# Low halves of h from PSUM by VectorE, GpSimd out of the weights' split, and an earlier first unit, in an attention and two mixture-of-experts layers on one core

## The chip, the core and the metric

The kernel runs on one core of a Trainium2 chip, as one program. The time is that of one launch on the device, in microseconds (us). The core has a matmul engine (TensorE, PE in the profile; PEld is its loading of weights), VectorE (DVE), ScalarE (ACT), GpSimd (POOL) and SyncE (SP), which here only starts transfers. Each engine works through its own queue in order; semaphores tie them together. SBUF is the on-chip memory that all of them read and write, PSUM the smaller one into which matmuls write.

## The reference

Attention over chunks of 32 tokens, then two layers of experts, all in float32 from and to DRAM:

```python
x = attention(q, k, v, mem_k, mem_v)         # 4 x 8 heads x 768 tokens x 64 -> 3072 tokens x 512
# first layer: each token goes to one of 8 experts, by the largest logits first, at most 384 to each
logits = x @ w_gate
for idx in argsort(-logits.flatten()):
    tok, e = idx // 8, idx % 8
    if assigned[tok] < 0 and counts[e] < 384:
        assigned[tok] = e; counts[e] += 1
for e in range(8):
    mask = assigned == e
    out[mask] = maximum(x[mask] @ w1[e], 0) @ w2[e]      # w1[e] 512 x 1024, w2[e] 1024 x 512
# second layer: each token goes to its best two of 8 experts, by noisy logits
noisy = x @ w_gate + log1p(exp(x @ w_noise)) * noise
top2, wt = top two of noisy, softmax over the two
for e in range(8):
    out[mask] += wt * (maximum(x[mask] @ w1[e], 0) @ w2[e])
```

The two layers have weights of their own. Tokens of the first layer depend on the gates of all tokens, and the second layer's gates on the first layer's outputs.

## The kernel before

Attention takes the first 165 us or so and is not touched but for a scale. Then an order of tokens is found (`route`), and the 16 experts follow, numbered k = 0 to 15: 0 to 7 are the first layer (called experts 0 to 7 here), 8 to 15 the second, in an order that depends on their load.

**One expert.** For the first layer 384 tokens are gathered by GpSimd's indirect DMAs into `xg`, and transposed by DMA into `xT`, as two float16 parts (high and low). `mm1` (L1168) computes 8 tiles of 128 of the 1024 hidden features: each is 12 matmuls, (high, high), (high, low) and (low, high) of weights and tokens, into one of three PSUM tiles (`tile1`). For k < KF = 5, the relu `hT` stays in float32 and the second matmul is in float32 too (`mm2_f32`), from the unsplit weights. From expert 5 on `hT` is also split: ScalarE writes the relu as float32 (`ht`) and as float16 (the high part), and `halve` (L1155) subtracts the two on GpSimd, or on VectorE if GpSimd is behind. `mm2` (L1205) then has 24 matmuls for each block of 128 tokens, 512 columns wide.

**The second layer.** An expert has up to 7 blocks of 128 slots, in two units: unit u = 2e with columns 0 to 3, the last a half block (448 slots), and u = 2e + 1 with columns 4 to 6 (384 slots). `lists2` and `list2` make the list of tokens of a unit by matmuls against one-hot rows (`slps<-slr,sloh`), `gathers2` fetches them, and `sums2` gathers the rows already in the output (`pv`), adds on VectorE and scatters them back. Unit 0 is special: its tokens come only from the first EARLY = 18 blocks of 128, that is the outputs of the first six experts, so that its list (`l1`) can be made while experts 6 and 7 still run. The list of unit 1 needs the gates of all 24 blocks (`M`, `rtqpos`). `gate_math` is run for the blocks in three groups: 0 to 11, 12 to 17, 18 to 23.

**Weights.** Each of the 32 weight matrices (i = 2k + m, m = 0 for w1) comes in four `st` tiles of 128 x 1024. ScalarE squares them, one matmul with ones (`tot`) makes the norm, from it VectorE makes a power-of-two scale, and `halves` (L1104) writes the high part by ScalarE and the low part in pieces: 256 columns by VectorE, or 512 by GpSimd as a multiplication and a subtraction. w2 of experts 0 to 4 is not split. In the profile these are `w_0h`, `w_0l` to `w_3h`, `w_3l`.

**What sets the order.** Nothing is placed by hand after the attention. `Pipe` (L73) keeps a modelled clock for each engine: each instruction goes through `Eng`, which adds its modelled cost in `account` (that is why all these instructions stand as L68 in the profile). The work around the matmuls is written as generators that yield a time or a condition. Between two matmuls `tick` runs each generator that is due, in the order of the list `gens`. `fits` lets VectorE take a piece when its clock is not ahead. Where PE needs something that by the model is not there, `until` and `wait` issue dummy matmuls (`m<-ones`) into the tile that is about to be used. So a changed cost in the model moves instructions on every engine.

Of the kernel before, what the change touches and what calls it, by code (L numbers as in the profile page):

```python
# [8 lines left out]
F32 = mybir.dt.float32  # L9
F16 = mybir.dt.float16  # L10
BF16 = mybir.dt.bfloat16
I32 = mybir.dt.int32
# [24 lines left out]
EARLY = CAP // 128 * (E - 2)  # L37
# [35 lines left out]
class Pipe:  # L73
# [9 lines left out]
    def __init__(self, nc):  # L83
        self.t = {k: 0.0 for k in "pvsgyd"}
        self.ready = {}
        self.due = 0.0
        self.early = set()
# [7 lines left out]
    def account(self, e, op, args, kw):  # L95
# [29 lines left out]
        elif e == "s":  # L125
            cost = (51.0 if ps else 93.0) + 94.0 * (ptr or "accum_out" in kw) + 0.833 * n
        else:
            cost = 147.0 + 1.887 * n if op == "tensor_tensor" else (245.0 if ptr else 122.0) + 0.832 * n
        end = self.t[e] = start + cost
# [26 lines left out]
    def add(self, gen, first=False):  # L156
        self.gens.insert(0 if first else len(self.gens), [gen, self.clock, False, None])
# [38 lines left out]
def pow2_scale(V_, pool, ssq, n, tag, keep=6, out=None):  # L196
# [5 lines left out]
    V_.tensor_scalar(s, t, -1.0, float(204 << 23), op0=ALU.mult, op1=ALU.add)  # L202
    V_.tensor_scalar(i, t, 1.0, float(50 << 23), op0=ALU.mult, op1=ALU.add)
# [17 lines left out]
def attention(ctx):  # L221
# [3 lines left out]
    with (  # L225
# [110 lines left out]
        def split(i):  # L336
# [4 lines left out]
            sx, ix = pow2_scale(nc.vector, wk, ssq, 1, "x", out=ixs[:, i : i + 1])  # L341
# [208 lines left out]
def positions(ctx, m, tag, between=(lambda: None,) * 2, counts=None):  # L550
# [11 lines left out]
    yield pipe.rdy("p", exc)  # L562
# [414 lines left out]
C_H = 2.0**-15  # L977
# [67 lines left out]
def split(ctx, i, st, eager):  # L1045
# [18 lines left out]
    def norms(js):  # L1064
        n = js.stop - js.start
        yield pipe.rdy("p", sq) + 1000
# [10 lines left out]
            i2[:, js].bitcast(I32), t[:, js], float(23 << 23), float(50 << 23), op0=ALU.max, op1=ALU.add  # L1077
# [26 lines left out]
    def halves(j, s):  # L1104
# [12 lines left out]
        fits = pipe.fits(395.0)  # L1117
        idle = lambda: (k == 0 or KF <= k <= E) and pipe.t["g"] <= pipe.clock + SLACKG
        a = 0
        while a < 1024:  # L1120
            yield lambda: fits() or idle()
            b = a + 256 if fits() else min(a + 512, 1024)
            if b == a + 256:
# [21 lines left out]
    if not eager:  # L1145
        s = yield from norms(slice(0, 4))
        if k < E:
            for j in reversed(range(4)):
                pipe.add(halves(j, s), True)
# [5 lines left out]
def halve(ctx, h, t, n, hT):  # L1155
    pipe = ctx.pipe
    yield pipe.rdy("g", h)
    fits = pipe.fits(69.0 + 1.04 * n)
    yield lambda: pipe.t["g"] <= pipe.clock + SLACKH or fits()
    (pipe.G if pipe.t["g"] <= pipe.clock + SLACKH else pipe.V).tensor_tensor(h[:, 1, :n], t, h[:, 0, :n], op=ALU.subtract)  # L1160
    hT.append(h)
# [6 lines left out]
def mm1(ctx, k, xT, n, ps, last=True):  # L1168

    pipe, W, hT = ctx.pipe, ctx.W[k], []  # L1170
    for ft in range(FT):
        if ft:
            ps = tile1(ctx)
# [20 lines left out]
        else:  # L1194
            t = ctx.wk.tile([128, n], F32, tag="ht", name="ht", bufs=3)
# [789 lines left out]
```

## Time and profile before

| | us |
|---|---|
| median of 3 runs | 1122.9 |
| lowest and highest | 1116.53 and 1127.39 |
| profiled execution, its own time | 1120.83 |
| its span in the trace | 1119.0 |
| mean granted clock of TensorE | 0.946 |
| attention and order of tokens, to the first expert's first matmul | 191.57 |
| experts 0 to 4, float32 second matmul | 229.92 |
| experts 5, 6, 7 | 40.20, 35.66, 48.67 |
| units 0, 1, 2 of the second layer | 53.07, 32.86, 43.34 |
| from unit 3 to the third last | 336.15 |
| last three units | 93.20 |
| tail | 14.36 |

The stages are cut at the first matmul of each expert or unit. Durations below are of the one profiled execution. [...] An idle time in brackets stands for the engine just before the instruction, with the instruction that it waited for.

### The profile page before, as it was taken

The numbers are of one execution on the slowest core, as the hardware profiler recorded it, in microseconds if no ns is written. First come the engines' busy times: TensorE is split into PE (matmuls) and PEld (weight loads), VectorE is DVE, ScalarE is ACT, GpSimd is POOL, SyncE is SP. The second block draws the span as 40 slices with busy tenths as digits, with TensorE's granted clock in tenths as the row PEclk, the third lists the DMA queues.
The fourth block names the chain that finished last, engine by engine and source line by source line (L and its number), as shares of the span: only waits on it lengthen the run. The fifth ranks groups of instructions, "written<-read, shape, count | busy, mean of one in ns | idle before, by whom it ended". The sixth has DMA issues, their size and how long they took to land. (4 is left out here: it accounts for less than half of the span.)

```text
span 1119.0 us, 21999 instructions
## 1 busy us (share of the span) xinstructions
PE 1000.2 (89%) x8051; PEld 598.2 (53%) x8051; DVE 730.9 (65%) x2337; ACT 495.0 (44%) x878; POOL 461.3 (41%) x589
## 2 busy tenths in 40 slices
PE   7767746999999998988978989999999999999994
PEld 6655634667676674444434435555455554555552
DVE  3676877878888889889685854827558374575100
ACT  1454523433524516885616815526255361643220
POOL 5455523301101225647434444544546444454531
PEclk8898966999999999998988999999999999999997
DMA  9999715456696758774538845637658364553510
GB/s 224 225 260 264 204 69 199 146 161 195 184 219 190 207 137 228 202 220 132 110 67 243 271 118 168 185 84 215 142 167 191 108 222 112 155 121 87 132 37 28
DMA packets 162657, 185.44 MB, mean 166 GB/s; under 512 B 108224, under 2 KB 120896, under 8 KB 162546
## 3 DMA queue, kind: packets, MB, share of 16 engines
q1 hardware_dynamic: 143856, 127.96, 44.6%
q0 software_dynamic: 15232, 49.75, 14.8%
q10 hardware_dynamic: 3458, 6.30, 1.6%
q8 instruction: 64, 1.05, 0.4%
q14 instruction: 47, 0.39, 0.1%
HBM read 127.14 MB, written 32.44 MB: 143 GB/s over the span
## 5 line engine op out<-in xcount | busy, mean ns | idle before, releaser
L68 PEld LDWEIGHTS <-hT 128*128 128x128 f16 (+2 forms) x1800 | 144.6, 100 | 183.4 <-issue 22.6
L68 ACT ACTIVATE ht<-m 128x384 f32<-128x384 f32 (+2 forms) x152 | 76.3, 502 | 255.0 <-PE m L68 230.6
L68 ACT ACTIVATE junk<-st 128x1024 f16<-128x1024 f32 x108 | 114.1, 1056 | 62.2 <-DVE sloh L68 22.6
L68 POOL TENSOR_TENSOR hT<-ht,hT 128x384 f16<-128x384 f32 (+2 forms) x121 | 117.2, 980 | 55.3 <-ACT hT L68 40.1
L68 DVE SCALAR_TENSOR_TENSOR pv<-m,ys,pv 128x512 f32<-128x512 f32 (+2 forms) x47 | 33.5, 714 | 148.5 <-PE m L68 148.1
L68 PE MATMUL m2f<-st,hT 128*128 128x256 f32 x480 | 124.7, 396 | 0.0
L68 POOL DMA_INDIRECT out_dram<-pv,ts x47 | 47.4, 1009 | 176.6 <-DVE pv L68 131.4
L68 POOL DMA_INDIRECT xg<-xr,idx x24 | 24.8, 1032 | 186.7 <-issue 95.4
L68 PE MATMUL m<-xT,w_3h 128*128 128x384 f16 (+2 forms) x384 | 99.6, 338 | 0.0
L68 PE MATMUL m<-xT,w_0h 128*128 128x384 f16 (+2 forms) x384 | 98.7, 337 | 0.0
L68 PE MATMUL m<-xT,w_2h 128*128 128x384 f16 (+2 forms) x384 | 97.0, 331 | 1.7 <-ACT hT L68 1.7
L68 PE MATMUL m<-xT,w_1h 128*128 128x384 f16 (+2 forms) x384 | 97.3, 333 | 0.0
L68 PEld LDWEIGHTS m2f<-st,hT 128*128 128x128 f32 x480 | 84.4, 190 | 10.0 <-ACT hT L68 0.3
L68 PE MATMUL m<-w_3h,hT 128*128 128x512 f16 (+2 forms) x300 | 72.5, 347 | 8.4 <-POOL hT L68 8.4
L68 PE MATMUL m<-w_0h,hT 128*128 128x512 f16 (+2 forms) x300 | 73.9, 354 | 2.9 <-ACT w_0h L68 2.9
L68 ACT ACTIVATE hT<-m 128x384 f16<-128x384 f32 (+2 forms) x152 | 75.9, 500 | 0.0
L68 PE MATMUL m<-w_1h,hT 128*128 128x512 f16 (+2 forms) x300 | 73.7, 351 | 0.0
L68 PE MATMUL m<-w_2h,hT 128*128 128x512 f16 (+2 forms) x300 | 73.0, 349 | 0.0
L68 DVE SCALAR_TENSOR_TENSOR w_1l<-st,s,w_1h 128x256 f16<-128x256 f32 x92 | 63.1, 728 | 13.2 <-ACT w_1h L68 13.2
L68 PE MATMUL m<-xT,w_3l 128*128 128x384 f16 (+2 forms) x192 | 65.0, 339 | 0.0
L68 PE MATMUL m<-xT,w_0l 128*128 128x384 f16 (+2 forms) x192 | 64.5, 336 | 0.0
L68 DVE SCALAR_TENSOR_TENSOR w_2l<-st,s,w_2h 128x256 f16<-128x256 f32 x102 | 61.9, 657 | 3.5 <-ACT w_2h L68 3.5
(339 smaller groups left out, 2128.1 us busy)
## 6 DMA issues: line engine op xcount, KB each, us to landing
st<-w_dram SPq DMA_DIRECT2D x64, 512.0 KB, 5.5
st<-x_dram SPq DMA_DIRECT2D x64, 512.0 KB, 4.5
v<-vctx_dram SPq DMA_DIRECT2D x24, 520.0 KB, 14.1
k<-kT_dram SPq DMA_DIRECT2D x24, 312.0 KB, 15.7
x<-rb SPq DMA_DIRECT2D x24, 264.0 KB, 2.5
q<-qT_dram SPq DMA_DIRECT2D x12, 512.0 KB, 17.4
out_dram<-zero ACTq DMA_DIRECT2D x24, 256.0 KB, 4.4
xr<-rb POOLq DMA_DIRECT2D x17, 264.0 KB, 7.6
```

Source lines behind the costliest of these rows:

```text
L68: return f(*args, **kw)
```

## The change

1. `halve`: for k from 5 on, ScalarE writes the high part only; VectorE computes max(PSUM, 0) minus the high part straight from the matmul's PSUM tile. GpSimd does it, from a float32 copy, only in the first layer when by the model VectorE is late and GpSimd free. `mm1` has a new `until`: a tile is begun only if at most two low parts are open.
2. `halves`: GpSimd takes part for k = 0 only; VectorE's pieces have 512 columns from k = 5 on.
3. `account`: a model of VectorE and GpSimd holding each other up when both work on two tensors in SBUF (`held`).
4. EARLY is 15 blocks, the outputs of five experts; the groups of `gate_math` become 0 to 8, 9 to 14, 15 to 23.
5. Order: `add` takes a rank (0 for `halve`, 1 for `halves` and the last two experts' `gate_rows`, else 2); `norms` waits 4000 ns of the model in place of 1000 for k from 5 on; the lists' matmuls of `l1` and `rtq` and the list of unit 0 and 1 come 2000 later.
6. Scales: powers of two are moved (TOPX, C_H), with no instruction more or less.

The low parts of h are 152 in number. Of these the order has 8 on GpSimd and 144 on VectorE after the change, where the profile has 121 on GpSimd and 31 on VectorE before. VectorE's weight pieces are 66 of 256 columns and 176 of 512, where 374 of 256 were; GpSimd's pairs 7 where 29 were. The dummies `m<-ones` are 106 where 55 were: 20 of the new ones stand ahead of expert 0, 31 ahead of unit 1.

```diff
-EARLY = CAP // 128 * (E - 2)
+EARLY = CAP // 128 * (E - 3)
...
+        if op in ("tensor_tensor", "scalar_tensor_tensor") and not ps:
+            if e == "g":
+                if self.t["v"] > start:
+                    start += 200.0
+                    self.t["v"] += cost
+                self.held = self.held[-3:] + [(start, start + cost)]
+            elif e == "v":
+                for a, b in self.held:
+                    if a - cost < start < b:
+                        start = b
         end = self.t[e] = start + cost
...
-    def add(self, gen, first=False):
-        self.gens.insert(0 if first else len(self.gens), [gen, self.clock, False, None])
+    def add(self, gen, rank=2):
+        at = sum(it[4] <= rank for it in self.gens)
+        self.gens.insert(at, [gen, self.clock, False, None, rank])
...
-def positions(ctx, m, tag, between=(lambda: None,) * 2, counts=None):
+def positions(ctx, m, tag, between=(lambda: None,) * 2, counts=None, late=0.0):
...
-    yield pipe.rdy("p", exc)
+    yield pipe.rdy("p", exc) + late
...
-C_H = 2.0**-15
+TOPX = 5
+C_H = 1.0
...
     def norms(js):
         n = js.stop - js.start
-        yield pipe.rdy("p", sq) + 1000
+        yield pipe.rdy("p", sq) + (1000 if k < KF else 4000)
...
-        fits = pipe.fits(395.0)
-        idle = lambda: (k == 0 or KF <= k <= E) and pipe.t["g"] <= pipe.clock + SLACKG
+        step = 512 if k >= KF else 256
+        fits = pipe.fits(129.0 + 1.04 * step)
+        idle = lambda: k == 0 and pipe.t["g"] <= pipe.clock + SLACKG
         a = 0
         while a < 1024:
             yield lambda: fits() or idle()
-            b = a + 256 if fits() else min(a + 512, 1024)
-            if b == a + 256:
+            dve = fits()
+            b = min(a + (step if dve else 512), 1024)
+            if dve:
                 V_.scalar_tensor_tensor(lo[:, a:b], src[:, a:b], sj, hi[:, a:b], op0=ALU.mult, op1=ALU.subtract)
...
 def halve(ctx, h, t, n, hT):
     pipe = ctx.pipe
-    yield pipe.rdy("g", h)
-    fits = pipe.fits(69.0 + 1.04 * n)
-    yield lambda: pipe.t["g"] <= pipe.clock + SLACKH or fits()
-    (pipe.G if pipe.t["g"] <= pipe.clock + SLACKH else pipe.V).tensor_tensor(h[:, 1, :n], t, h[:, 0, :n], op=ALU.subtract)
+    if t.space == PSUM:
+        yield pipe.rdy("v", h) - 100
+        pipe.V.scalar_tensor_tensor(h[:, 1, :n], t, 0.0, h[:, 0, :n], op0=ALU.max, op1=ALU.subtract)
+    else:
+        yield pipe.rdy("g", h)
+        pipe.G.tensor_tensor(h[:, 1, :n], t, h[:, 0, :n], op=ALU.subtract)
     hT.append(h)
...
         if ft:
+            pipe.until(lambda: len(hT) > ft - 3)
             ps = tile1(ctx)
...
-            t = ctx.wk.tile([128, n], F32, tag="ht", name="ht", bufs=3)
-            pipe.S.activation(t, ps, AF.Relu, scale=C_H)
-            pipe.S.activation(h[:, 0, :n], ps, AF.Relu, scale=C_H)
-            pipe.add(halve(ctx, h, t, n, hT))
+            pipe.S.activation(h[:, 0, :n], ps, AF.Relu)
+            t = ps
+            if k < E and pipe.t["v"] > pipe.clock + SLACKH and pipe.t["g"] <= pipe.clock + SLACKH:
+                t = ctx.wk.tile([128, n], F32, tag="ht", name="ht", bufs=3)
+                pipe.S.activation(t, ps, AF.Relu)
+            pipe.add(halve(ctx, h, t, n, hT), 0)
...
-    ps = yield from slot_list(ctx, pi, na, 128, ids, LATE * (e > 0))
+    ps = yield from slot_list(ctx, pi, na, 128, ids, LATE if e else 2000.0)
...
-    pp = yield from positions(ctx, m0, "l1")
+    pp = yield from positions(ctx, m0, "l1", late=2000.0)
...
-    pp = yield from positions(ctx, ctx.M2, "rtq", counts=cnt)
+    pp = yield from positions(ctx, ctx.M2, "rtq", counts=cnt, late=2000.0)
```

Three places in the order of the instructions. The first is unit 2. GpSimd's queue at its end, before the change (`pv_4` to `pv_6` are the rows gathered for the sums of unit 3's columns, `hT` the low parts of unit 2's h):

```order
L68 TENSOR_TENSOR hT<-ht,hT 128x448 x2
L68 DMA pv_4_9497<-out_dram,tg_3_9488 128x512
L68 DMA pv_5_9499<-out_dram,tg_3_9488 128x512
L68 DMA pv_6_9508<-out_dram,tg_3_9488 128x512
L68 TENSOR_TENSOR hT<-ht,hT 128x448
L68 DMA out_dram<-pv_0_9347,ts_2_9084 3072x512
```

VectorE's queue in the same unit, after (the pieces of `w_3l` are the weights of a later expert, `m_9090` to `m_9201` five of the unit's PSUM tiles):

```order
L68 SCALAR_TENSOR_TENSOR hT<-m_9090,hT 128x448
L68 SCALAR_TENSOR_TENSOR w_3l<-st_3_8619,s_19_9057,w_3h 128x512
L68 SCALAR_TENSOR_TENSOR hT<-m_9118,hT 128x448
L68 SCALAR_TENSOR_TENSOR hT<-m_9155,hT 128x448
L68 SCALAR_TENSOR_TENSOR hT<-m_9177,hT 128x448
L68 TENSOR_SCALAR nt_9222<-tot_9220 128x4
L68 SCALAR_TENSOR_TENSOR hT<-m_9201,hT 128x448
```

The subtractions have left GpSimd's queue and stand on VectorE between the weight pieces.

The second is the matmuls for the positions of all tokens (`rtqpos`, `cnt`, from VectorE's `M_69`), on PE in unit 0. Before:

```order
L68 LDWEIGHTS w_3h
L68 MATMUL m_8445<-xT_0_8005,w_3h 128x448
L68 LDWEIGHTS tri_791
L68 MATMUL rtqpos<-M_69,tri_791 128x192
L68 LDWEIGHTS ones_64
L68 MATMUL rtqpos<-rtqexc,ones_64 128x192
L68 LDWEIGHTS ones_64
L68 MATMUL cnt_8426<-rtqexc,ones_64 128x8
L68 LDWEIGHTS ones_64
L68 MATMUL cnt_8426<-M_69,ones_64 128x8
L68 LDWEIGHTS w_3l
L68 MATMUL m_8445<-xT_0_8005,w_3l 128x448
```

and after:

```order
L68 LDWEIGHTS hT
L68 MATMUL m_8368<-w_2l,hT 128x512
L68 LDWEIGHTS tri_791
L68 MATMUL rtqpos<-M_69,tri_791 128x192
L68 LDWEIGHTS ones_64
L68 MATMUL rtqpos<-rtqexc,ones_64 128x192
L68 LDWEIGHTS ones_64
L68 MATMUL cnt_8385<-rtqexc,ones_64 128x8
L68 LDWEIGHTS ones_64
L68 MATMUL cnt_8385<-M_69,ones_64 128x8
L68 LDWEIGHTS hT
L68 MATMUL m_8368<-w_3h,hT 128x512
```

They moved from the last tile of `mm1` to the first block of `mm2`, behind 18 of its matmuls.

The third is PE's queue at the end of unit 0. Before, the last matmul of the list, then the norm of weights (`tot`), and the half block of `mm2`:

```order
L68 LDWEIGHTS sloh
L68 MATMUL slps<-slr,sloh 128x21
L68 LDWEIGHTS onesb
L68 MATMUL tot_8807<-sq_8670,onesb 128x4
L68 LDWEIGHTS hT
L68 MATMUL m_8726<-w_3l,hT 64x256
L68 LDWEIGHTS hT
L68 MATMUL m_8726<-w_3l,hT 64x256
```

After, the last two of 31 dummies and the start of unit 1 (`xT_1`), which come right behind the half block:

```order
L68 LDWEIGHTS ones_64
L68 MATMUL m_8677<-ones_64 128x128
L68 LDWEIGHTS ones_64
L68 MATMUL m_8677<-ones_64 128x128
L68 LDWEIGHTS w_0h
L68 MATMUL m_8677<-xT_1_8537,w_0h 128x384
L68 LDWEIGHTS w_0h
L68 MATMUL m_8677<-xT_1_8537,w_0h 128x384
L68 LDWEIGHTS w_0l
L68 MATMUL m_8677<-xT_1_8537,w_0l 128x384
```

`tot` left this place (it stands in unit 1's `mm1` now), and the dummies came.

## Rows read from the trace of the kernel before

**Rows 1.** The page, part 1: busy time and share by engine, whole span.
```profile
...
PE 1000.2 (89%) x8051; PEld 598.2 (53%) x8051; DVE 730.9 (65%) x2337; ACT 495.0 (44%) x878; POOL 461.3 (41%) x589
...
```

**Rows 2.** Windows by stage: stretch, length, busy time by engine, PEclk, DMA.
```profile
...
421.49:461.69 40.20, 35.78 (x230) 18.59 (x229) 36.76 (x103) 28.88 (x54) 24.62 (x34) 0.92 0.93 247
461.69:497.35 35.66, 32.31 (x197) 16.99 (x196) 30.45 (x78) 31.59 (x61) 20.29 (x20) 1.00 0.65 199
497.35:546.02 48.67, 39.40 (x224) 19.37 (x223) 38.80 (x137) 27.19 (x49) 25.02 (x24) 0.86 0.56 139
546.02:599.09 53.07, 42.25 (x287) 21.72 (x286) 38.73 (x117) 17.30 (x33) 22.16 (x20) 0.90 0.42 120
599.09:631.95 32.86, 32.86 (x172) 17.04 (x172) 24.29 (x64) 26.37 (x43) 14.72 (x15) 0.95 0.84 232
631.95:675.29 43.34, 39.45 (x243) 19.93 (x241) 25.90 (x67) 13.74 (x26) 22.89 (x20) 0.96 0.49 144
675.29:1011.44 336.15, 330.06 (x2151) 173.63 (x2150) 196.14 (x481) 157.19 (x280) 161.57 (x160) 1.00 0.57 156
706.47:744.90 38.43, 37.55 (x243) 19.44 (x242) 21.99 (x56) 12.78 (x25) 19.83 (x19) 1.00 0.56 161
1011.44:1104.64 93.20, 93.20 (x504) 49.23 (x503) 22.39 (x48) 25.07 (x52) 39.10 (x41) 1.00 0.29 80
...
```

**Rows 3.** Timeline of PE, experts 5 to 7: start, length, work, idle before.
```profile
...
441.40 0.59 PE L68 MATMUL m<-w_0h,hT 128*128 128x512 f16 x2 [2.94 <-ACT w_0h L68]
...
502.38 0.18 PE L68 MATMUL l1pos<-M,tri 128*128 128x18 f16 x1 [2.43 <-DVE M L68]
...
540.96 0.39 PE L68 MATMUL lg<-wg2hl,yT 128*128 128x32 f16 x8 [2.13 <-DMA yT<-rb]
...
```

**Rows 4.** Timeline of PE, units 0 to 2, and unit 6.
```profile
...
565.52 0.32 PE L68 MATMUL rtqpos<-M,tri 128*128 128x192 f16 x1 [4.94 <-DVE M L68]
...
575.51 0.75 PE L68 MATMUL slps<-slr,sloh 128*128 128x9 f16 x24
...
597.89 0.16 PE L68 MATMUL tot<-sq,onesb 128*128 128x4 bf16 x1 [5.22 <-ACT junk L68]
...
659.97 0.39 PE L68 MATMUL m<-w_3h,hT 128*128 128x512 f16 x1 [2.63 <-POOL hT L68]
...
800.62 0.39 PE L68 MATMUL m<-w_3h,hT 128*128 128x512 f16 x1 [1.71 <-POOL hT L68]
...
```

**Rows 5.** Windows behind the wait that ended at 659.97, columns as in rows 2.
```profile
...
660.00:664.00 4.00, 4.00 (x11) 1.49 (x12) 0.75 (x1) 0.00 (x0) 1.03 (x1) 0.57 0.15 51
...
```

**Rows 6.** Tile views of hT, pv, rb: durations as min/median/max in ns.
```profile
...
L68 POOL TENSOR_TENSOR hT<-ht,hT x121: 902/931/1482, 425.5 to 1090.6; 128x384 f16<-128x384 f32 x86, 128x448 f16<-128x448 f32 x18, 128x416 f16<-128x416 f32 x17
...
L68 DVE TENSOR_TENSOR hT<-ht,hT x31: 545/578/1261, 517.8 to 1059.4; 128x384 f16<-128x384 f32 x18, 128x416 f16<-128x416 f32 x7, 128x448 f16<-128x448 f32 x6
...
L68 DVE SCALAR_TENSOR_TENSOR pv<-m,ys,pv x47: 349/751/752, 660.6 to 1105.1; 128x512 f32<-128x512 f32 x42, 128x128 f32<-128x128 f32 x3, 128x256 f32<-128x256 f32 x2
...
L68 DVE SCALAR_TENSOR_TENSOR rb<-y,y_s,rb x48: 384/476/1377, 244.4 to 549.2; 128x256 f16<-128x256 f32 x48
...
L344 DVE SCALAR_TENSOR_TENSOR rb<-x,x_s,rb x2: 750/750/750, 145.7 to 147.3; 128x512 f16<-128x512 f32 x2
...
```

**Rows 7.** Timeline of POOL in unit 2.
```profile
...
654.99 1.36 POOL L68 DMA_INDIRECT pv<-out_dram,tg  x1 [3.17 <-DVE xw L68]
...
```

**Rows 8.** DVE's groups by form, experts 5 to 7: busy, mean ns, idle.
```profile
...
L68 DVE SCALAR_TENSOR_TENSOR w_2l<-st,s,w_2h 128x256 f16<-128x256 f32 x24 | 19.9, 883 | 0.0
...
```

**Rows 9.** Timeline of POOL and of DVE in unit 0.
```profile
...
549.83 1.20 POOL L68 TENSOR_TENSOR w_1l<-st,w_1h 128x512 f16<-128x512 f32 x1
...
550.08 1.23 DVE L68 SCALAR_TENSOR_TENSOR w_1l<-st,s,w_1h 128x256 f16<-128x256 f32 x1
...
```

**Rows 10.** Timeline of SP, the transposes into unit 1's xT.
```profile
...
580.33 5.53 SPq L68 DMA_TRANSPOSE xT<-xg  x3
...
```

**Rows 11.** Tile view of xT, its last line.
```profile
...
DMA to landing us min/median/max: 2.5/5.0/10.3
```

More of the change, by code (lines that the diff above doesn't have):

```diff
@@ L86, in __init__ @@
         self.due = 0.0
+        self.held = []
         self.early = set()
@@ L193, in until, with pow2_scale @@
             assert n < 100000, [(g[0].__name__, g[1], g[3]) for g in self.gens]
-def pow2_scale(V_, pool, ssq, n, tag, keep=6, out=None):
+def pow2_scale(V_, pool, ssq, n, tag, keep=6, out=None, top=15):
     t = pool.tile([128, n], I32, tag=tag + "_t", name=tag + "_t")
@@ L201, in pow2_scale @@
     V_.tensor_scalar(t, ssq.bitcast(I32), 24, 23, op0=ALU.logical_shift_right, op1=ALU.logical_shift_left)
-    V_.tensor_scalar(s, t, -1.0, float(204 << 23), op0=ALU.mult, op1=ALU.add)
-    V_.tensor_scalar(i, t, 1.0, float(50 << 23), op0=ALU.mult, op1=ALU.add)
+    V_.tensor_scalar(s, t, -1.0, float(204 - 15 + top << 23), op0=ALU.mult, op1=ALU.add)
+    V_.tensor_scalar(i, t, 1.0, float(50 + 15 - top << 23), op0=ALU.mult, op1=ALU.add)
     return s.bitcast(F32), i.bitcast(F32)
@@ L340, in split @@
             hl = rb[:, :DM].bitcast(F16)
-            sx, ix = pow2_scale(nc.vector, wk, ssq, 1, "x", out=ixs[:, i : i + 1])
+            sx, ix = pow2_scale(nc.vector, wk, ssq, 1, "x", out=ixs[:, i : i + 1], top=TOPX)
             nc.vector.tensor_scalar(hl[:, :DM], xf, sx, None, op0=ALU.mult)
@@ L1076, in norms @@
         V_.tensor_scalar(
-            i2[:, js].bitcast(I32), t[:, js], float(23 << 23), float(50 << 23), op0=ALU.max, op1=ALU.add
+            i2[:, js].bitcast(I32), t[:, js], float(23 << 23), float(50 + (TOPX if m == 0 else 0) << 23),
+            op0=ALU.max, op1=ALU.add,
         )
@@ L1147, in split @@
         if k < E:
-            for j in reversed(range(4)):
-                pipe.add(halves(j, s), True)
+            for j in range(4):
+                pipe.add(halves(j, s), 1)
         else:
@@ L1309, in gate_rows @@
     yield pipe.rdy("v", ssq)
-    s, i = pow2_scale(V_, wk, ssq, na, f"y{na}", keep=3)
+    s, i = pow2_scale(V_, wk, ssq, na, f"y{na}", keep=6, top=TOPX)
     V_.tensor_scalar(ctx.iy[:, NA * k + a0 : NA * k + a0 + na], i, ctx.iwg2, None, op0=ALU.mult)
@@ L1426, in gates @@
                 yield lambda: all((k, a) in ctx.Y for a in p)
-                pipe.add(gate_rows(ctx, k, [(a, ctx.Y.pop((k, a))) for a in p]), k >= E - 2)
+                pipe.add(gate_rows(ctx, k, [(a, ctx.Y.pop((k, a))) for a in p]), 1 if k >= E - 2 else 2)
     def maths():
```

## The prediction

> **What bounds the kernel now.** I read the shares of the page first: TensorE (PE) is busy for 1000.2 of 1119 us, VectorE (DVE) for 730.9 [rows 1]. So the time is PE's own work plus what PE waits, and the wins can only lie in the waits. The windows by stage say where they are [rows 2]. The floor of a stage comes from the last three units of MoE2, in which PE never idles at full clock: 93.20 / 3 = 31.07 us for one expert block of 384 tokens. It is made of 96 matmuls of 384 columns and 72 of 512, so by columns one takes 31.07 / (96 + 72 x 4/3) = 0.162 us, a 512 one 0.216, a dummy of 128 columns 0.054, one of 448 columns 0.189.
>
> Against that floor the stages lose:
> - Experts 5, 6 and 7 take 40.20 + 35.66 + 48.67 = 124.5 us. With their gate logits and list matmuls I count 33 each (2 over the floor, an estimate), so 25.5 are lost.
> - Unit 0 takes 53.07; a later unit of the same 448 columns took 38.43 (the window from 706.47 in [rows 2]): 14.6 lost. Unit 1 loses 32.86 - 31.07 = 1.8, unit 2 loses 43.34 - 38.43 = 4.9.
> - From unit 3 on PE idles 336.15 - 330.06 = 6.1 us.
>
> Sum: 53. What PE waits for there, in the order of time: a split weight from ScalarE (2.94), VectorE's M (2.43), a transposed row of the gate by DMA (2.13) [rows 3]; again M (4.94), the squares of the next weights' norm (5.22), and the low part of h from GpSimd, 2.63 in unit 2 and 1.71 in a later unit; three more such in units 4, 8 and 10 are 0.88, 1.70 and 1.49 long [rows 4]. [...]
>
> **h's low parts.** Before, ScalarE writes the relu of each tile twice and GpSimd subtracts in 121 of 152 cases, 0.93 us each, VectorE in 31, 0.58 [rows 6]. GpSimd is in order: in unit 2 the last subtraction stood behind three gathers of rows for the sums, of which the first waited 3.17 us for VectorE's xw and began at 654.99; PE went on at 659.97 [rows 4, 7]. The order shows that behind this no GpSimd work on h is left in MoE2 (8 pieces remain, in MoE1). So the waits for it, 2.63 and 0.88 + 1.71 + 1.70 + 1.49 = 5.8, go, and with the first its 1.7 of low clock. What is late next is the `dup` matmul of unit 2, 1 us, which stays in my account.
>
> VectorE gets 144 subtractions from PSUM in place of 31 from SBUF. No row shows just this one. Nearest: VectorE's `pv`, also two tensors with one in PSUM, 0.751 for 512 columns, and its `rb` piece from SBUF alone, 0.750 for 512 and 0.476 for 256 [rows 6], which makes 1.07 ns a column. So 384 columns from PSUM should take 0.751 - 128 x 1.07 ns = 0.61 us, 448 ones 0.68; the ends are 0.48 (a 256 piece) and 0.75 (a 512 one), and I take the slope, since 384 and 448 lie between. 144 x 0.62 = 90 us come to VectorE, 31 x 0.58 = 18 leave. [...]
>
> **The weights' split.** VectorE's 374 pieces of 256 columns become 66 of 256 and 176 of 512, and GpSimd's pairs fall from 29 to 7, all in expert 0. A piece of 256 takes 0.476 at the median (rb, of the same shape), but in experts 5 to 7 the mean of w_2l is 0.883 [rows 6, 8]: I take the difference for pieces that ran beside GpSimd. At 550.08 one took 1.23 while GpSimd's subtraction of 1.20 ran from 549.83 [rows 9]. After: 66 x 0.476 + 176 x 0.750 = 163 us, against 178 for 374 clean pieces, and more for those that paid. With GpSimd gone from weights and h, I expect the clean price in experts 5 to 7. [...]
>
> In experts 5 to 7 VectorE was busy for 36.76 + 30.45 + 38.80 = 106 of 124.5 us [rows 2], 50 of them in 66 weight pieces (w_2l's 24 are the first of four such groups [rows 8]). After: 24 weight tiles of two pieces, 24 x 1.50 = 36, and 24 x 0.61 = 15 for h: 106 - 50 + 36 + 15 = 107, if the gates and lists keep their contended prices, and about 91 if every instruction that the order has there gets the clean price of its form. PE's floor is 99. I take it to be nearer to 91, since GpSimd has only row copies and gathers left there: it fits, but narrowly. So the waits for VectorE and for split weights shrink and do not vanish. What stays: waits for the gate's rows by DMA (2.13 is one), part of the wait for lists, and the low clock behind each. I put 10 us for what is left of 25.5 (3.5 of DMA, 3 of lists, 3.5 of clock): a gain of 15.5. The ends are 20 (only the DMA waits and their clock stay) and 6 (VectorE's list work ends last as it does now).
>
> **Early unit from 15 blocks, and the later list.** The order has the early unit's list in the middle of expert 7's mm1 in place of its end, and the matmul for M (`rtqpos`) no longer inside unit 0's mm1 but 18 matmuls into its mm2. M came 19.5 us after unit 0's start (565.52 - 546.02). Now its group of gates has 9 blocks where it had 6, and eight subtractions stand ahead of it on VectorE, so I put M at 24. PE is there at 18.6 + 18 x 0.216 = 22.5, so 1.5 to 2 us of wait are left of 4.94. Then come 0.9 for the second matmul and 39 x 0.216 = 8.4 of mm2, and the list's matmuls stand at 33.3 to 34.0. From them the next unit's rows go by GpSimd's gathers and three transposes on SP. Before, it took from 575.51 to 585.86 until the last of the three was issued [rows 4, 10], 10.35; a transpose lands 2.5 to 10.3 after its issue begins [rows 11], and I put 12.7 for the whole. So xT of unit 1 is there at 34.0 + 12.7 = 46.7. PE has in the meantime 15 matmuls (3.2), the half block (2.7) and the 31 dummies that the planner now puts there (1.7), to about 42, then 4 to 5 us idle and some 2 at half clock. The wait of 5.22 for `tot` is gone: `tot` now stands in unit 1's mm1. Unit 0 and 1 together: 46.7 + 2 + 31.1 = 80 against 85.9, a gain of 6 where 16.4 were lost. Ends: 0 (M at 30) and 10 (rows in 10 us).
>
> **Others.** 20 dummies more ahead of the first expert's mm1: they lie on PE, 20 x 0.054 = 1.1 us lost if xT was there, nothing if not. ScalarE loses 144 activations, off PE's path but in experts 5 to 7, where a wait for it is among the 25.5: nothing more. The new `until` on two open low parts issues no dummy in MoE2 but those counted. The changed scales change no instruction count.
>
> **Sum.** 15.5 (experts 5 to 7) + 6 (units 0, 1) + 3.4 (unit 2: 4.9 less 1.5 that stay) + 5.8 (later units) - 1.1 = 29.6. The profiled execution took 1120.8 (span 1119.0), 2.1 less than the median of 1122.9: 1120.8 - 29.6 = 1091, or 1093 beside the median. I take **1090**.
>
> **Rivals.**
> - A, the waits go nearly all: 20 + 10 + 4.9 + 5.8 = 41, so 1080, or 1070 when the gate's DMA waits go too, being earlier. For it: GpSimd's hold on VectorE is seen in many rows. Against: the DMA chain of unit 1 does not depend on VectorE's speed.
> - B, VectorE becomes the bound in experts 5 to 7. If it needs the 107 of the upper end, with its own idles beside that, MoE1 and unit 0 gain nothing and the rest gains 9: 1112.
> - C, slower: the PSUM tiles. There are three for mm1; each is now held until VectorE has read it, no longer until ScalarE has. PE runs two tiles, 2 x 12 x 0.162 = 3.9 us, ahead before it stands. ScalarE and VectorE take at most pv's 0.75 each, 1.5, so VectorE must be late by 2.4 us: more than three clean pieces of 512 in a row. If each of the 24 tiles of experts 5 to 7 and half of MoE2's 128 lose 0.5 us, that is 44, more than the gain: 1135. For it: lists of 6 x 0.7 us come in rows on VectorE. Against: the subtraction goes first in the queue.
> - D, the change does not do what it says: pieces of 512 stay slow, at 1.3 us, for another cause than GpSimd. That is 176 x 0.55 = 97 us more on VectorE, which has 100 us idle in MoE2 but none before: gain of 9 lost again, about 1120.
>
> **How the numbers follow.** Chances: the forecast (1080 to 1100) 0.55; A (1070 to 1080) 0.13; B (1100 to 1115) 0.18; C 0.06; D 0.08. The forecast alone spans 1080 to 1100 by the ends of experts 5 to 7 and units 0 and 1; with A and most of B the range is 1070 to 1112. About 1% (11 us) is what a measurement of this kernel, whose runs lie 1116.5 to 1127.4, can tell from no change. Faster by more: forecast, A and most of B, 0.83; within: rest of B, D, 0.11; slower: C, 0.06.
>
> **What would show it.** Right: no wait for GpSimd's hT; pieces of 512 at a median of 0.75 with few above 1; subtractions from PSUM of 0.6 to 0.7; experts 5 to 7 near 110 us; the wait ahead of unit 1 named xT and 4 us long. Wrong: waits in mm1 for a PSUM tile released by VectorE (C); VectorE busy all through experts 5 to 7 with PE waiting for it (B); subtractions over 0.8 us.

## The result and the profile after

The changed kernel takes 1089.73 us at the median of 4 runs (1088.29 to 1095.11), the kernel before 1124.87 in the runs beside it. The ratio is 0.971, with a 95% interval of 0.968 to 0.9741: faster by 2.6 to 3.2%. The profiled execution took 1089.54, its span is 1087.7, 31.3 us less than before.

The page's shares of the span by engine, of the changed kernel [against rows 1]:

```profile
...
PE 989.5 (91%) x8099; PEld 596.5 (55%) x8099; DVE 687.1 (63%) x2317; ACT 438.2 (40%) x734; POOL 305.4 (28%) x432
...
```

PE is busy for 10.7 us less with 48 matmuls more, which I take for matmuls that no longer run at the lower clock (mean granted clock 0.957, before 0.946). VectorE has 44 us less although it does 144 subtractions for 31: 730.9 to 687.1. GpSimd falls from 461.3 to 305.4.

The windows of the same stages, cut again at the first matmul of each expert or unit, of the changed kernel (columns as in rows 2): experts 5, 6, 7, units 0, 1, 2, then all from unit 3 on, and the last three units.

```profile
...
420.81:456.31 35.50, 33.89 (x253) 18.47 (x252) 27.70 (x91) 25.84 (x46) 12.13 (x20) 1.00 0.99 223
456.31:490.91 34.60, 32.76 (x215) 17.52 (x214) 29.91 (x113) 26.84 (x50) 1.82 (x2) 1.00 0.78 231
490.91:525.69 34.78, 33.05 (x219) 17.52 (x217) 27.75 (x94) 24.96 (x43) 8.42 (x8) 1.00 0.82 197
525.69:570.30 44.61, 40.33 (x294) 21.93 (x293) 37.02 (x121) 11.56 (x20) 7.67 (x7) 1.00 0.30 78
570.30:603.99 33.69, 33.69 (x196) 17.61 (x197) 17.27 (x57) 19.88 (x31) 6.60 (x7) 0.95 0.82 259
603.99:641.39 37.40, 37.40 (x244) 19.55 (x243) 27.07 (x76) 18.34 (x30) 13.02 (x12) 1.00 0.75 204
641.39:979.90 338.51, 331.91 (x2151) 173.83 (x2150) 176.10 (x459) 126.53 (x200) 108.04 (x105) 1.00 0.61 158
979.90:1073.11 93.21, 93.21 (x505) 49.22 (x503) 27.21 (x60) 15.83 (x28) 20.48 (x21) 1.00 0.32 77
...
```

By stage, from these and [rows 2]:

| | before | after | gain | forecast |
|---|---|---|---|---|
| start, to expert 0 | 191.57 | 194.39 | -2.8 | -1.1 |
| experts 0 to 4 | 229.92 | 226.42 | 3.5 | 0 |
| experts 5 to 7 | 124.5 | 104.9 | 19.6 | 15.5 |
| units 0 and 1 | 85.9 | 78.3 | 7.6 | 6 |
| unit 2 | 43.3 | 37.4 | 5.9 | 3.4 |
| unit 3 on, before the last three | 336.15 | 338.51 | -2.4 | 5.8 |

The granted clock is 1.00 in experts 5 to 7 and in unit 0, where it was 0.86 to 0.92 in three of the four stages. What PE still waits for, its timeline in the changed kernel (start, length, work, idle before):

```profile
...
438.39 0.36 PE L68 MATMUL lg<-wg2hl,yT 128*128 128x32 f16 x8 [1.61 <-DMA yT<-rb]
...
468.09 0.48 PE L68 MATMUL m<-xT,w_2h 128*128 128x384 f16 x2 [1.64 <-DVE hT L68]
...
548.16 0.25 PE L68 MATMUL rtqpos<-M,tri 128*128 128x192 f16 x1
...
558.03 0.75 PE L68 MATMUL slps<-slr,sloh 128*128 128x9 f16 x24
...
570.30 0.48 PE L68 MATMUL m<-xT,w_0h 128*128 128x384 f16 x2 [3.20 <-DMA xT<-xg]
...
807.52 0.59 PE L68 MATMUL m<-w_0h,hT 128*128 128x512 f16 x2 [2.01 <-DVE pv L68]
...
```

A gate's row by DMA (1.61, and a second of the kind in expert 7), a tile in expert 6 for which VectorE's `hT` was late (1.64), and xT of unit 1 by DMA (3.20). `rtqpos`, which waited 4.94 for M [rows 4], waits for nothing. The last line is new: in unit 7 PE stands 2.01 us for VectorE's `pv`, because `pv` reads the PSUM tile that the next block needs.

VectorE's groups by form, over the whole span of the changed kernel (busy, mean ns of one, idle before):

```profile
...
L68 DVE SCALAR_TENSOR_TENSOR hT<-m,hT 128x384 f16<-128x384 f32 x96 | 53.0, 553 | 70.0 <-ACT hT L68 67.1 <-issue 2.8
...
L68 DVE SCALAR_TENSOR_TENSOR w_1l<-st,s,w_1h 128x512 f16<-128x512 f32 x44 | 31.3, 745 | 2.9 <-ACT w_1h L68 2.9
...
L68 DVE SCALAR_TENSOR_TENSOR hT<-m,hT 128x448 f16<-128x448 f32 x24 | 14.9, 619 | 11.7 <-ACT hT L68 8.7 <-ACT junk L68 2.0 <-issue 0.9
...
```

The subtraction of 384 columns takes 0.553 us and of 448 columns 0.619; a weight piece of 512 takes 0.745 in the group `w_1l`, and 0.745 to 0.769 in the four groups. The wait of PE in unit 7 is explained by VectorE's own timeline there:

```profile
...
804.46 0.17 DVE L68 COPY meta<-xg 128x2 f32<-128x2 f32 x1 [4.17 <-DMA xg<-x,rows]
...
806.72 1.41 DVE L68 SCALAR_TENSOR_TENSOR pv<-m,ys,pv 128x512 f32<-128x512 f32 x2
...
```

VectorE stood 4.17 us for a gathered row `xg` from which it copies two columns (`meta`), with two weight pieces and the sum `pv` queued behind. Over the whole kernel this adds up, in the view of the waits of VectorE (us in total, times, longest):

```profile
...
DVE meta L68 <- DMA xg<-x,rows: 25.7, 15, 4.2
...
```

Before, the same copies waited once, for 1.0 us. And ScalarE has waits that it did not have, its timeline at the end of unit 4's mm1:

```profile
...
696.26 0.54 ACT L68 ACTIVATE hT<-m 128x448 f16<-128x448 f32 x1 [5.71 <-remote]
...
```

PE had finished that tile at 692.24. The trace names no work that released it ("remote"). There are six such waits, 25.8 us together.

### The profile page after: what moved, and what is told of

Its sections match the earlier page's. It is cut to its first block, busy times and chain, and to the rows that moved or that the text cites. A ratio compares the mean times of both kernels' runs of the same rounds, so it can differ in the third digit from the quotient of the medians.

```text
span 1087.7 us, 21508 instructions
## 1 busy us (share of the span) xinstructions
PE 989.5 (91%) x8099; PEld 596.5 (55%) x8099; DVE 687.1 (63%) x2317; ACT 438.2 (40%) x734; POOL 305.4 (28%) x432
## 5 line engine op out<-in xcount | busy, mean ns | idle before, releaser
L68 DVE SCALAR_TENSOR_TENSOR hT<-m,hT 128x384 f16<-128x384 f32 (+2 forms) x144 | 82.0, 570 | 109.3 <-ACT hT L68 96.1
L68 POOL DMA_INDIRECT out_dram<-pv,ts x47 | 52.9, 1126 | 254.7 <-DVE pv L68 126.0
L68 PE MATMUL m<-xT,w_3h 128*128 128x384 f16 (+2 forms) x384 | 96.5, 331 | 0.0
L68 DVE SCALAR_TENSOR_TENSOR pv<-m,ys,pv 128x512 f32<-128x512 f32 (+2 forms) x47 | 33.3, 712 | 86.3 <-PE m L68 86.1
L68 PE MATMUL m<-w_1h,hT 128*128 128x512 f16 (+2 forms) x300 | 71.3, 345 | 0.0
L68 PE MATMUL m<-xT,w_1l 128*128 128x384 f16 (+2 forms) x192 | 63.6, 331 | 0.0
L68 PE MATMUL m<-xT,w_2l 128*128 128x384 f16 (+2 forms) x192 | 63.5, 331 | 0.0
L68 POOL DMA_INDIRECT pv<-out_dram,tg x47 | 46.4, 986 | 56.7 <-DMA out_dram<-pv,ts 22.1
```

What stands on the lines that cost most here:

```text
L68: return f(*args, **kw)
```

## The experiments

Each was timed against the kernel before on the same chip, in three groups of four; the medians of that kernel were 1120.3, 1117.5 and 1120.3. Ratios are to it. Between groups the ratio of one kernel can differ, as the second run of the changed kernel shows.

### The copies of the gathered columns later

```diff
-METAS = 8000.0
+METAS = 16000.0
```

> The changed kernel with the copies of the gathered rows' meta columns placed 16000 ns of the model behind the gather, not 8000. My theory: the term for the later units failed (2.4 us lost where 5.8 were to be won) because VectorE, in order, waits 25.7 us in 15 places for those gathers to land, with subtractions, weight pieces and sums behind. Then these waits fall below 5 us, PE's 1.3 and 2.2 us waits for pv (units 3 and 7) go, and the time is 1083 to 1087. Rival, the later units lose because VectorE has the low parts of h to do at all: the waits for the gathers may go, the time stays at 1088 to 1092.

1079.17 us, ratio 0.965 (0.9616 to 0.9685). VectorE's waits:

```profile
...
DVE meta L68 <- DMA xg<-x,rows: 4.1, 3, 2.1
...
```

PE's waits for `pv` are gone, and from unit 3 on it took 422.9 to the last matmul against 432.1 in the first profile of the change. So the waits were what the theory says. In the stage from unit 3 to before the last three, which the prediction counted, the gain against the kernel before is 6.9 us here. The gain in total is larger than expected, but only a part of it belongs to the copies, as the next experiment shows. The stages show something else: expert 6 took 39.1 here against 34.6, at code that the edit does not touch. Timeline of ScalarE and of PE there, in this kernel:

```profile
...
456.31 1.06 ACT L68 ACTIVATE junk<-st 128x1024 f16<-128x1024 f32 x1 [3.62 <-DMA st<-w_dram]
...
464.16 0.58 PE L68 MATMUL m<-xT,w_2h 128*128 128x384 f16 x2 [3.56 <-DVE hT L68]
...
```

ScalarE stood 3.62 us for a weight's DMA, with the relu of a tile queued behind it; VectorE got the high part late and then had seven weight pieces in a row before it came to the next two subtractions; PE stood 3.56 us for the PSUM tile. That is rival C's mechanism, in one place. ScalarE's stand is not needed for it: in the first profile of the change ScalarE stands for no weight there, the same seven pieces stand in a row on VectorE, and PE waits 1.64. The end of that row, VectorE's timeline in the change:

```profile
...
466.83 0.74 DVE L68 SCALAR_TENSOR_TENSOR w_3l<-st,s,w_3h 128x512 f16<-128x512 f32 x1
467.49 1.01 DVE L68 SCALAR_TENSOR_TENSOR hT<-m,hT 128x384 f16<-128x384 f32 x2
...
```

### The changed kernel once more

No edit.

> The changed kernel once more, for a second profile. In its first profile units 3 to 11 took 9 us more than with the later meta copies; of these some 3.5 are sums that waited behind VectorE's wait for a gather, and some 5 are late low parts in units 4, 6, 8 and 10, where ScalarE stood 5.3 to 6.0 us with no releaser in the trace. If the cause of both is the place of the copies, as my theory has it, both come again: VectorE waits over 15 us for gathers, units 3 to 11 take 303 to 308. Rival: ScalarE's stalls are of one execution and not of the program; then units 4 to 10 take 1.3 us less each here, with the waits for gathers still there. The time is 1086 to 1091 by either.

1082.76 us, ratio 0.9673 (0.963 to 0.9715). The rival on ScalarE was right: none of its waits without a releaser came again, and units 4, 6, 8 and 10 took 37.38, 34.97, 34.98 and 34.77 where the first profile has 38.09, 36.19, 36.23 and 36.55. So the 5.0 us of these four units belong to one execution, and so do ScalarE's stands; what they were stays open. The waits for gathers did come again, first VectorE's, then PE's:

```profile
...
DVE meta L68 <- DMA xg<-x,rows: 15.4, 10, 2.8
...
```

```profile
...
PE m L68 <- DVE pv L68: 2.8, 1, 2.8
...
```

The wait in expert 6 came again too, and longer: 3.41 us, behind the same seven pieces, after ScalarE had stood 2.43 for a weight. PE's waits for `hT`:

```profile
...
PE m L68 <- DVE hT L68: 3.6, 2, 3.4
...
```

Expert 6 took 38.0 here, at a granted clock of 0.96, and experts 5 to 7 together 109.2, where the first profile has 104.9.

From unit 3 on to the last matmul this profile has 426.3, so the copies cost 426.3 - 422.9 = 3.4 us, in unit 3 nearly all (34.12 against 31.18). The time of 1079.2 with later copies and 1082.8 without stand in different groups, with intervals that overlap: the gain of that edit is shown in the stage, not in the total.

### Without the model of VectorE and GpSimd holding each other up

The lines of `held` in `account` are left out.

> The changed kernel without the model of VectorE and GpSimd holding each other up; by the order it has 20 dummies fewer ahead of expert 0 and 18 in place of 31 ahead of unit 1. My theory: the model is what puts the first expert's matmul 2.8 us later, and with GpSimd nearly out of the way it gains nothing elsewhere: expert 0 starts near 191.6, the whole takes 1086 to 1090. Rival, the model carries part of the gain of experts 5 to 7, since the planner no longer puts work where it is slow: these three lose 5 us or more and the time is 1093 or above.

1092.15 us, ratio 0.9746 (0.9705 to 0.9788). It starts expert 0 at 191.16, but the profiles of this study start it between 187.99 and 196.15, also where code and order up to there are the same; so no profile can show what 20 dummies cost, and the term "start" of the sum cannot be tested. Experts 5 to 7 took 113.3, 8.4 more than in the first profile of the change and 4.1 more than in the second, about the rival's 5. VectorE's pieces cost the same there (0.745), so these three experts were slower by the order and not by slower pieces. The time lies between the two ranges, its interval overlaps that of the change, and more is not to be said.

### Weight pieces of 256 columns

```diff
-        step = 512 if k >= KF else 256
+        step = 256
```

> The changed kernel with VectorE's weight pieces of 256 columns throughout; PE's and GpSimd's order stay as they are but for the dummies ahead of unit 1. A clean pair of 256 pieces takes 0.95 us, one of 512 0.75, so VectorE has 176 x 0.20 = 35 us more, 10 of them in experts 5 to 7. My theory: VectorE fits only narrowly there, so experts 5 to 7 and unit 0 lose 4 to 10 us: 1094 to 1100. Rival: VectorE has slack, the pieces are hidden and the time stays within 3 us of 1090.

1085.36 us, ratio 0.9694 (0.9662 to 0.9725): my theory falls for the total and for experts 5 to 7, and the time lies below the rival's range too, which ended at 1087. These experts took 103.4, the least of all profiles, with pieces at 0.476 to 0.500 us. Unit 0 did lose, as it had it: five waits of 0.56 to 1.16 us for VectorE's weight pieces, and unit 1 one of 4.7; together 8.5 more (86.8). So experts 5 to 7 lose nothing by the shorter pieces. The `meta` copies, at 8000 as in the change, wait only 2.0 us in all in this order.

### GpSimd reading beside VectorE

```diff
                 V_.scalar_tensor_tensor(lo[:, a:b], src[:, a:b], sj, hi[:, a:b], op0=ALU.mult, op1=ALU.subtract)
+                if KF <= k < E:
+                    scr = ctx.rt.tile([128, 512], F16, tag="scr", name=f"scr{i}_{j}_{a}")
+                    ctx.nc.gpsimd.tensor_tensor(scr, src[:, a:b], hi[:, a:b], op=ALU.subtract)
```

> The changed kernel with one GpSimd subtraction of 512 columns from SBUF, into a tile that nobody reads, behind each of VectorE's weight pieces of experts 5 to 7; the planner does not count it, so the order of all other work stays. My theory, that VectorE's slowness before came from GpSimd reading SBUF beside it: the pieces of these weights rise from 0.75 to 1.2 us or more on the mean, the subtractions of h from PSUM stay at 0.55 to 0.60, and experts 5 to 7 and unit 0 lose 10 us or more together: 1100 to 1112. Rival, the pieces were slow for another cause: they stay at 0.75 and the time at 1088 to 1092.

1113.6 us, a little above my range, ratio 0.9953 (0.9924 to 0.9983): more than four fifths of the gain are lost to 48 operations whose results nobody reads. VectorE's groups by form in experts 5 to 7 of this kernel, then GpSimd's, then PE's waits for `hT`:

```profile
...
L68 DVE SCALAR_TENSOR_TENSOR w_2l<-st,s,w_2h 128x512 f16<-128x512 f32 x12 | 18.4, 1567 | 0.0
...
L68 DVE SCALAR_TENSOR_TENSOR w_3l<-st,s,w_3h 128x512 f16<-128x512 f32 x12 | 10.6, 897 | 0.0
L68 DVE SCALAR_TENSOR_TENSOR hT<-m,hT 128x384 f16<-128x384 f32 x16 | 8.6, 543 | 1.8 <-ACT hT L68 1.8
...
```

```profile
...
L1146 POOL TENSOR_TENSOR scr<-st,w_2h 128x512 f16<-128x512 f32 x10 | 13.6, 1364 | 0.7
...
```

```profile
...
PE m L68 <- DVE hT L68: 13.0, 4, 8.1
...
```

The pieces of `w_2l` rose from 0.745 to 1.567, those of `w_0l` and `w_1l` from 0.827 and 0.743 to 1.234 and 1.361, `w_3l` least, from 0.790 to 0.897. In the trace the 48 pieces fall into two kinds: 29 overlap a subtraction on GpSimd and took 1.61 us in the mean, 19 overlap none and took 0.741, the longest of them 0.751. The subtraction from PSUM took 0.543, as in the change (0.545 in these experts); 8 of the 16 overlap GpSimd, and these took 0.545. Experts 5 to 7 took 131.8 where the change has 104.9 and 109.2, and PE stood up to 8.1 us for a PSUM tile that VectorE had not read. The order of everything else is the same, and GpSimd's own work behind the added subtractions explains little: what PE waited for GpSimd's `hT` is 1.3 us. This is the cleanest proof of the study.

### GpSimd back in the split

```diff
-        idle = lambda: k == 0 and pipe.t["g"] <= pipe.clock + SLACKG
+        idle = lambda: (k == 0 or KF <= k <= E) and pipe.t["g"] <= pipe.clock + SLACKG
```
and without the model of VectorE and GpSimd holding each other up.

> The changed kernel with GpSimd back in the split of the weights for experts 5 to 7 and the first expert of the second layer (some 22 pairs more), and without the model of VectorE and GpSimd holding each other up, so that the planner does it as before. To be read against the run without that model alone, 1092. My theory, each pair holds a piece of VectorE: the pieces' mean in experts 5 to 7 is 0.9 or more, the stretch loses 5 to 15 us against that run: 1097 to 1107. Rival, GpSimd takes work off VectorE and this outweighs the hold: 1085 to 1092.

1101.17 us, ratio 0.9875 (0.9819 to 0.9931), against 0.9746 (0.9705 to 0.9788) without that model alone: 1.3% or 14 us, as my theory has it (the medians, of two groups, are 9 us apart). Experts 5 to 7 took 118.9 against 113.3, experts 0 to 4 2.4 more; PE's two longest waits in experts 5 to 7 are 5.0 and 5.6 us, both for VectorE's `hT`. One of the four groups of pieces there, by form:

```profile
...
L68 DVE SCALAR_TENSOR_TENSOR w_2l<-st,s,w_2h 128x512 f16<-128x512 f32 x9 | 9.8, 1110 | 0.0
...
```

`w_0l` and `w_1l` are at 1.10 and 1.05, `w_3l` at 0.746.

### h's low parts as before

`halve` and the lines of `mm1` that call it are those of the kernel before; all else is changed.

> The changed kernel with h's low parts done as before: ScalarE writes the relu twice, GpSimd subtracts in 133 cases, VectorE in 19; all else as changed. My theory, h on GpSimd both holds VectorE's pieces up and puts the low part behind gathers in GpSimd's queue: pieces of 512 in experts 5 to 7 rise above 0.85 us on the mean, these experts lose 5 to 12 us, and PE waits for GpSimd's hT in the even units of the second layer again, 4 to 6 us in all: 1098 to 1108. Rival, the weights' split carries the gain and h does not matter: 1086 to 1092.

1105.41 us, ratio 0.9882 (0.9843 to 0.9921), 22.6 us above the changed kernel in the same group. The size is more than I expected, and the place is another: the pieces in experts 5 to 7 stayed at 0.74 to 0.80 (I had said over 0.85), and these experts took 111.5 against 109.2. The loss is in the second layer, where units 0 to 2 took 8.7 us more together, and units 7 and 11 39.6 and 40.3 in place of 31.2 (this profiled execution is 10 us over the median, so it shows the places and not the sizes). Timelines of GpSimd, ScalarE and PE in unit 7 of this kernel:

```profile
...
807.29 1.01 POOL L68 DMA_INDIRECT out_dram<-pv,ts  x1 [3.51 <-DMA out_dram<-pv,ts]
...
813.39 3.51 POOL L68 TENSOR_TENSOR hT<-ht,hT 128x384 f16<-128x384 f32 x4
...
814.34 0.49 ACT L68 ACTIVATE ht<-m 128x384 f32<-128x384 f32 x1 [12.00 <-POOL hT L68]
...
814.37 0.61 PE L68 MATMUL m<-w_1h,hT 128*128 128x512 f16 x1 [5.57 <-POOL hT L68]
...
```

GpSimd's scatter waited for an earlier scatter to land, then came four gathers, and only then the subtractions. ScalarE stood 12.0 us for a free `ht` tile, PE 5.57 us for a low part. That is [rows 7] in a worse form.

### The early unit from 18 blocks

```diff
-EARLY = CAP // 128 * (E - 3)
+EARLY = CAP // 128 * (E - 2)
```

> The changed kernel with the early unit again from 18 blocks. By the order the planner puts 123 dummies (6.7 us) at the end of expert 7 and ahead of unit 0, in place of 31 (1.7) ahead of unit 1. My theory, the early unit from 15 blocks is what takes the list's wait out of the stretch from expert 7 to unit 1: that stretch loses 5 to 12 us, 1094 to 1102. Rival, it only moves the wait from unit 0 to unit 1: 1087 to 1091.

1089.52 us, ratio 0.9748 (0.9694 to 0.9803), 6.8 us above the changed kernel of the same group, with intervals that overlap. From expert 7 to unit 1 it took 42.3 + 38.1 + 38.0 = 118.4 against 34.7 + 44.7 + 33.6 = 113.0. So the wait is in part moved (unit 0 is 6.6 faster, expert 7 7.6 slower), in part won; the stretch loses 5.4 us, the low end of my theory. That is one profile of this kernel; the two of the change have 113.1 and 113.0. The total stands in the rival's range, since both ranges were set beside 1089 and the kernel without this edit took 1083 here.

### Three edits to the kernel with later copies

The first puts ScalarE's squares of the weights of experts 5 to 7 later, the second has weight pieces of 256 columns for these experts only, the third has both:

```diff
-        yield max(pipe.rdy("s", st[j]), pipe.t["s"] - 100)
+        yield max(pipe.rdy("s", st[j]) + (5000 if KF <= k < E else 0), pipe.t["s"] - 100)
```

> The kernel with the meta copies at 16000, and ScalarE's squares of the weights of experts 5 to 7 placed 5000 ns of the model later. In experts 5 to 7 PE stood up to 3.7 us in expert 6 at the start of a tile, for a PSUM tile that VectorE had not read; VectorE had waited for ScalarE, and ScalarE had stood 3.6 us for a weight's DMA with the relu queued behind. My theory, ScalarE's in-order wait for the weights is the first cause: with the squares later it falls below 1 us, expert 6 takes 34 to 35.5, and the end of expert 7 comes 3 to 5 us earlier: 1074 to 1078. Rival, the weights' arrival itself bounds experts 5 to 7, so what expert 6 gains expert 7 or 5 loses: 1078 to 1082.

1089.99 us, ratio 0.9743 (0.9695 to 0.979). PE's stand in expert 6 is gone (35.3). But the edit moves the weight pieces as well, which come after the squares: five stand in a row on VectorE during expert 6's `mm1` now, where seven stood. So it is not shown which of the two, the row or ScalarE's wait for the weights, was the cause. Expert 4 took 3.6 and expert 7 3.9 more, with a wait of 1.41 for `hT` there, and the time rose: the rival's direction, and worse than its range.

```diff
-        step = 512 if k >= KF else 256
+        step = 512 if k >= E else 256
```

> The kernel with the meta copies at 16000, and VectorE's weight pieces of 256 columns for experts 5 to 7, 512 for the second layer. With 256 columns everywhere these experts took 103.4 and units 0 and 1 lost 8. If shorter pieces let a subtraction of h in between and that is what helps, experts 5 to 7 take 102 to 105 and the time is 1074 to 1078. Rival, the 103.4 was the start of the first expert and the weights' arrival: 1078 to 1082.

1079.4 us, ratio 0.9644 (0.9593 to 0.9695): the rival. Experts 5 to 7 took 105.8, and the time is that of the later copies alone.

> Both of these edits on the kernel with the meta copies at 16000. If each takes its own wait away, experts 5 to 7 take 100 to 103 and the time is 1071 to 1076; if the weights' DMA bounds them, 1077 to 1082.

1094.12 us, ratio 0.9783 (0.9724 to 0.9842): above both ranges; expert 6 alone took 49.2. The longest of PE's waits there is for the squares of a norm, behind stands of ScalarE of 4.70 and 2.83 us for a weight's DMA:

```profile
...
PE tot L68 <- ACT junk L68: 4.7, 2, 4.3
...
```

Why the two together lose so much more than each alone was not followed further.

### h by VectorE from SBUF

In `mm1` ScalarE writes the relu in float32 too, always, and `halve` subtracts the two on VectorE.

> The kernel with the meta copies at 16000, and all of h's low parts by VectorE, but from a float32 copy in SBUF that ScalarE writes, as before the change, so that the PSUM tile is free when ScalarE has read it. ScalarE has 152 activations of 0.5 us more. If the hold of the PSUM tile is what PE waits for in expert 6, the waits at a tile's start fall below 1 us and the time is 1074 to 1078. Rival, reading from PSUM is as cheap and the hold costs nothing that ScalarE's second activation would not cost as well: the low parts take 0.54 to 0.60 us here too, the time is 1079 to 1086.

1092.46 us, ratio 0.9764 (0.9714 to 0.9813). The low parts cost the same from SBUF, 0.559 us at the median against 0.558 from PSUM in the change, in the tile view of `hT`:

```profile
...
L68 DVE TENSOR_TENSOR hT<-ht,hT x152: 547/559/626, 421.2 to 1060.7; 128x384 f16<-128x384 f32 x104, 128x448 f16<-128x448 f32 x24, 128x416 f16<-128x416 f32 x24
...
```

PE waits nowhere for a PSUM tile held by VectorE (once, 1.8, for one held by ScalarE), and the kernel is slower all the same: units 0 and 1 took 87.1 against 78.6, with waits of 2.6 for M and 5.3 for VectorE in unit 1. So the hold of the PSUM tile is not what this kernel would win by giving up; that the second activation and its tile cost the difference is not shown, since the order moved as well. The time is above the rival's range too.

## Why the prediction was right

The forecast was 1090, the result is 1089.7, and in the same execution the sum of 29.6 stands against 31.3. The hit is closer than the terms deserve: the forecast gains of experts 0 to 7 and units 0 to 2 were too small, and that of the later units too large. In the order of the table the terms missed by -1.7, +3.5, +4.1, +1.6, +2.5 and -8.2 us, and that these add up to +1.8 is luck.

**h's low parts, price.** Worked out as 0.61 and 0.68 us from the price of `pv` and a slope, measured 0.553 and 0.619 in the mean: 82.0 us for 144 instead of 90. The slope was right (1.03 ns a column for 1.07), the fixed part of `pv` was too large a model.

**The weights' split.** 0.750 was forecast for a piece of 512, and 0.745 to 0.769 measured, by group. In experts 5 to 7 three of 48 pieces took 0.93 to 1.73 us; all three overlap one of the 8 subtractions of h that the order left on GpSimd, which the prediction did not count there. That GpSimd was the cause of [rows 9] is shown by the two kernels in which it comes back: their pieces are slow again (1.05 to 1.11 us in three of four groups with GpSimd back in the split, 0.90 to 1.57 with its idle subtractions), and their times 14 and 24 to 31 us longer than their partners'.

**Experts 0 to 4.** The 3.5 us that I had not in the sum are in part a shift: PE is busy for 1.7 us less there, 40 matmuls fewer stand in that stretch (1510 for 1550), and 36 more in experts 5 to 7 (687 for 651). The rest is less idle time.

**Experts 5 to 7.** VectorE was busy for 27.70 + 29.91 + 27.75 = 85.4 us, below the 91 of the lower end, so rival B did not come. The gain of 19.6 lies at the upper end of 6 to 20 because the 3.5 us of low clock that I had left in did not come: behind waits of 1.61, 1.64 and 1.22 us the granted clock stayed at 1.00. The second profile has 109.2, a gain of 15.3: its waits are 2.59, 3.41 and 1.15 us, and in the 4 us behind the 3.41 the granted clock was 0.66, between 1.00 and the 0.50 that the trace of the kernel before has from 661 to 663 us. So part of this term lies in one execution and not in the program. No run shows the 3.5: by the missing share of the clock, 0.34 of 4 us, the second profile has 1.4 behind that wait, an estimate, and the first profile none. The 1.7 of low clock that the prediction puts behind unit 2's wait is worked out in the same way, 0.43 of the 4 us of [rows 5]. With the start before it, both end expert 7 at the same point of the span, 525.7 and 525.9, 20.3 and 20.1 us earlier than before, where the terms up to there sum to 14.4. In the three profiles with the same order up to there the start lies between 187.99 and 194.39 and the end between 524.1 and 525.9. That the weights' DMA sets this point is likely (its share is 0.78 to 0.99 there, and ScalarE waits for it), but not shown.

**Units 0 and 1.** 6 forecast, 7.6 and 7.7 measured. M was no longer late at all: `rtqpos` stood at 548.16, 22.5 us after the unit's start, where PE was forecast to be at 22.5. The list's matmuls came 32.3 us after the start (33.3 to 34.0 forecast), and xT 12.3 after them (12.7 forecast): the wait that I named is there, 3.20 where 4 to 5 were forecast. The 2 us at half clock behind it came to 1.7, by the same estimate: the granted clock was 0.57 in the 4 us from 570.30. That the unit also gains time with 15 blocks in place of 18 is borne out at 5.4 us by the stages; the 6.8 of the totals are not clear of their intervals.

**Unit 2.** It gained 5.9, more than the 4.9 that I counted as lost; the 1.5 that I left for the `dup` matmul and its clock did not stay (PE 37.40 of 37.40 us busy, granted clock 1.00).

**Later units: the step that failed.** "So the waits for it, 2.63 and 0.88 + 1.71 + 1.70 + 1.49 = 5.8, go": they went, and I put nothing in their place. In the profile shown units 3 to 11 lost 2.4 us. VectorE, in the new order, came to the copies of `meta` before the gathers had landed, and what was queued behind, the sums, became PE's wait. This costs 3.4 us by the second profile, which gains 3.4 there in place of 5.8; with the copies later the gain was 6.9. The two profiles of the change differ by 5.8 us in this stage, and 5.0 of it lie in the four units in which ScalarE had its waits in one execution.

**Rival C**, the hold of the PSUM tile, is real and small here: one place in expert 6, 1.64 us in the profile shown, 3.41 in the second profile, 3.56 with later copies, and 8.1 where GpSimd holds VectorE up. In the first three seven weight pieces stand in a row on VectorE there; the prediction asked for more than three. **Rival D** fell with the prices.

## What to carry to other kernels

An engine that helps can cost more than it does: 48 idle subtractions of GpSimd from SBUF cost this kernel 24 us against one run of the change and 31 against the other, mainly through VectorE's weight pieces with two inputs in SBUF (1.61 us beside GpSimd, 0.741 otherwise), while the subtraction with one input in PSUM was untouched (0.545 beside GpSimd, 0.543 over all). When work leaves a queue, look at what moves forward in it: here a copy that waits for a gather came too early, stood up to 4.17 us at the head of an in-order queue, and took back half of a term (3.4 us, where 6.9 were gained with the copy later). And where a start moves by 6 us between executions while a later point stays, compare stages from fixed points, not a single stage's length.

## What was not expected of the hardware

- Single idles of PE of 1.2 to 2.8 us left the granted clock at 1.00 (experts 5 to 7 and unit 7 of the change; in its second profile also in the 4 us behind idles of 2.59 in expert 5 and 2.78 in unit 3). Behind the idle of 3.20 ahead of unit 1 it was 0.57 in the next 4 us, behind the 3.41 in expert 6 of the second profile 0.66. In the kernel before it was 0.57 behind a 2.63 that had another idle, of 1.08, some 4 us ahead of its end.
- In one execution ScalarE stood 5.3 to 6.0 us in four units, in unit 4 beyond the end of the matmul that it waited for by 4.0 us, with no releaser in the trace; the second profile of the same program has none of it. Its cause is open.
- When h was on GpSimd, one of its scatters into DRAM began only when an earlier scatter had landed, after 3.51 us of idle, with four gathers behind it. The kernel before has five such waits, 14.0 us together.
